# The V store of head 30 as an indexed GpSimd store without eight rows, and x and grad_out loaded to all partitions

## The chip, the cores and the metric

The kernel runs on one core of a Trainium2 chip. Five engines each work through their own list of instructions: TensorE (PE; its weight loads are shown as PEld), VectorE (DVE), ScalarE (ACT), GpSimd (POOL) and SyncE (SP). They are ordered only by semaphores. SyncE, ScalarE and GpSimd can each issue DMAs; all of these are carried by the same 16 DMA engines. In the profile the DMA packets of SyncE are queue q1, those of ScalarE q10, those of GpSimd q0.

The metric is the device time of one execution in microseconds, as the median of several runs. Beside it stands the profile of one execution. All times given as points in time are microseconds from the start of that execution's span.

## The reference, cut to what matters

The reference computes one decoding step of a transformer block, and the gradients of all its inputs. A layer-normed row x (640 numbers) goes through attention against a cache of 8192 keys and values for each of 32 heads, and beside it through a gated MLP. Cut and simplified:

```python
def _A_ref(x, k_cache, v_cache, wq, wo):
    q = (x @ wq).reshape(B, Sq, Hq, Dh).transpose(0, 2, 1, 3)
    scores = jnp.einsum("bhqd,bhkd->bhqk", q, k) * (Dh ** -0.5)
    p = _softmax(scores, axis=-1)
    o = jnp.einsum("bhqk,bhkd->bhqd", p, v)
    return o.transpose(0, 2, 1, 3).reshape(B, Sq, Hq * Dh) @ wo
...
def _B_ref(x, w1, w3, w2):
    h = _silu(x @ w1) * (x @ w3)
    return h @ w2
...
x = A_x
xn = _layernorm(x, axis=-1)
return x + _A_ref(xn, A_k_cache, A_v_cache, A_wq, A_wo) + _B_ref(xn, B_w1, B_w3, B_w2)
...
_out, _vjp = jax.vjp(_f, A_x, A_k_cache, A_v_cache, A_wq, A_wo, B_w1, B_w3, B_w2)
_grads = _vjp(grad_out)
return (_out, *_grads)
```

All tensors are bfloat16. The caches and their gradients have the shape (1, 32, 8192, 128): 2 MB for K and 2 MB for V of each head. With one query, the gradient of K of one head is the outer product of a vector over the 8192 positions with one over the 128 columns, and so is that of V. So the kernel must read 134 MB of caches and write 134 MB of their gradients; the weights and their gradients add some 17 MB each way (the page counts 151.34 MB read and as many written).

## The kernel before, in words

Head by head, one K tile and one V tile are loaded by SyncE (2 MB each, 128 partitions of 64 positions, that is 16 KB in one piece on each partition). TensorE transposes them in pieces (`T`, L305), ScalarE copies these out of PSUM (L307), TensorE multiplies them with q and with the head's part of the gradient (`Mp`, L324), and the scores and the gradient of the probabilities come out of small products (`selm`, L340). Softmax, then `o_sum` and `dq_sum` (L417) use the tiles once more. At last DVE overwrites the tiles in place with the outer products (`outer`, L450): `outer_v` with the gradient of V, `outer_k` with that of K. `store` (L461) sends the tile to HBM, gives its buffer back and calls `load_next`, which issues the next load if there is one.

There are ten such buffers (`NSLOT`). Four of them hold the MLP's weights in the first part of the run and join the others later. All loads and stores of K and V go through one function, `fifo` (L105), so they stand in one list on SyncE, in the order in which the code calls it; a store that waits for DVE holds back all that stand behind it.

The outer products of head h are made while head h+1 is computed: `outers_a(h)` makes the whole of V and stores it, and makes half of K; `outers_b(h)` makes the other half of K and stores it. So the last stores on SyncE are V28, K28, V29, K29, V30, K30, V31, K31 (a letter for the cache and the number of the head). The 64 loads have all been issued before V28 is stored.

Heads come in groups of four. The weights wq and wo of a group are loaded, and their gradients stored, by GpSimd (L111, L113, L495, L504). The last group's two stores (0.64 MB each) end the kernel together with K31, and four small stores of the output row and of x's gradient by ScalarE (L813).

At the start, x and grad_out are each loaded as one row into one partition (L99). TensorE turns them into columns (L219, L221) and spreads grad_out over all partitions (L223, L225); ScalarE copies that into `g_bc` (L227, L228). The mean and the variance of x are sums over a column and then over the partitions (L231 to L237). The normalised column `xn_col_bf` goes into the first q (`prep_q`, L260). `g_bc` goes into the first products with wo (`prep_do`, L251), for which the group's wo must have landed.

Nothing in the code says which instruction waits for which. A layer below it derives the waits from what each instruction reads and writes, tiles and tensors in HBM alike. DMAs are counted on a few semaphores in turn (lanes): eight for SyncE and ScalarE together, eight for GpSimd. A DMA that takes a lane first waits until the one before it on that lane has landed. The instructions stand on each engine in the order in which the code makes them.

Of the kernel before, what the change touches and what calls it, by code (L numbers as in the profile page):

```python
# [9 lines left out]
BF16 = mybir.dt.bfloat16  # L10
F32 = mybir.dt.float32
ALU = mybir.AluOpType
ACTF = mybir.ActivationFunctionType
AX = mybir.AxisListType
PSUM = bass.MemoryType.PSUM

P = 128
# [4 lines left out]
def kernel(  # L22
# [22 lines left out]
    nc = tc.nc  # L45
    H = A_k_cache.shape[1]
    SK = A_k_cache.shape[2]
    DH = A_k_cache.shape[3]
    D = A_x.shape[2]
    F = B_w1.shape[1]  # L50
    assert DH == P and D % P == 0 and SK % P == 0
    NC = D // P
# [5 lines left out]
    scale = float(DH) ** -0.5  # L58

    consts = ctx.enter_context(tc.tile_pool(name="consts", bufs=1))  # L60
    kvpool = ctx.enter_context(tc.tile_pool(name="kv", bufs=1))
    wpool = ctx.enter_context(tc.tile_pool(name="wp", bufs=3))
    tpool = ctx.enter_context(tc.tile_pool(name="tp", bufs=4))
# [12 lines left out]
    dkc = out_2.rearrange("b h (p j) d -> (b h) p (j d)", p=P)  # L76
    dvc = out_3.rearrange("b h (p j) d -> (b h) p (j d)", p=P)
# [14 lines left out]
    NSLOT = 10  # L92
    RW = 64

    rows_in = []
    for src in (A_x, grad_out):
        r_kt = tpool.tile([P, 4, P], F32, name="row_kt", tag="KT")
        row = r_kt[0:1].rearrange("p k w -> p (k w)").bitcast(BF16)[:, 0:D]
        nc.scalar.dma_start(row, src.rearrange("a b d -> (a b) d"))  # L99
        rows_in.append(row)  # L100
    x_row, g_row = rows_in
    g_bc = consts.tile([P, D], BF16, name="g_bc")

    def fifo(out_, in_):
        nc.sync.dma_start(out_, in_)  # L105
# [16 lines left out]
    def load_next():  # L122
        if not pending or len(free_slots) < lag[0]:
            return
        kind, h = pending.pop(0)
        t = free_slots.pop(0)
        fifo(t[:], (kc if kind == "K" else vc)[h])
        kv_tiles[(kind, h)] = t
# [33 lines left out]
    ident_f = consts.tile([P, P], F32, name="ident_f")  # L162
    make_identity(nc, ident_f[:])
    ident_bf = consts.tile([P, P], BF16, name="ident_bf")
    nc.vector.tensor_copy(ident_bf[:], ident_f[:])
    masks = consts.tile([P, 4], F32, name="masks")
    pm_one = masks[:, 0:2]
    nc.vector.memset(pm_one[:, 0:1], 1.0)
    nc.vector.memset(pm_one[:, 1:2], -1.0)
    ones_b = pm_one[:, 0:1].to_broadcast([P, P])  # L170
    negones_b = pm_one[:, 1:2].to_broadcast([P, P])
    one_bf = consts.tile([P, 1], BF16, name="one_bf")
    nc.vector.memset(one_bf[:], 1.0)
    eps_t = consts.tile([P, 1], F32, name="eps_t")
# [22 lines left out]
    negmean = consts.tile([P, 1], F32, name="negmean")  # L197
    rstd = consts.tile([P, 1], F32, name="rstd")
    x_col = consts.tile([P, NC], F32, name="x_col")
    g_col = consts.tile([P, NC], F32, name="g_col")  # L200
    xn_col = consts.tile([P, NC], F32, name="xn_col")
    xn_col_bf = consts.tile([P, NC], BF16, name="xn_col_bf")

    def kt_tile():
        return tpool.tile([P, 4, P], F32, name="KT", tag="KT")

    def t_tile():
        t = kt_tile()
        return t[:].rearrange("p k w -> p (k w)").bitcast(BF16)

    def pst():
        return ps_t.tile([P, 512], F32, name="pT", tag="pT")

    ln3 = consts.tile([P, 3], F32, name="ln3")
    xsum, sumsq, std = ln3[:, 0:1], ln3[:, 1:2], ln3[:, 2:3]
    ps_xg = pst()
    ps_g = pst()
    for ci in range(NC):
        nc.tensor.matmul(ps_xg[:, ci:ci + 1], lhsT=x_row[:, ci * P:(ci + 1) * P], rhs=one_bf[0:1, :],  # L219
                         start=True, stop=True)  # L220
        nc.tensor.matmul(ps_xg[:, NC + ci:NC + ci + 1], lhsT=g_row[:, ci * P:(ci + 1) * P], rhs=one_bf[0:1, :],  # L221
                         start=True, stop=True)
    nc.tensor.matmul(ps_xg[:, P:P + D - 512], lhsT=one_bf[0:1, :].to_broadcast([1, P]), rhs=g_row[:, 512:D],  # L223
                     start=True, stop=True)
    nc.tensor.matmul(ps_g[:], lhsT=one_bf[0:1, :].to_broadcast([1, P]), rhs=g_row[:, 0:512],  # L225
                     start=True, stop=True)
    nc.scalar.copy(g_bc[:, 0:512], ps_g[:])  # L227
    nc.scalar.copy(g_bc[:, 512:D], ps_xg[:, P:P + D - 512])  # L228
    nc.vector.tensor_copy(x_col[:], ps_xg[:, 0:NC])
    nc.vector.tensor_copy(g_col[:], ps_xg[:, NC:2 * NC])  # L230
    nc.vector.tensor_reduce(xsum, x_col[:], AX.X, ALU.add)  # L231
    nc.tensor.matmul(ps_xg[:, 16:17], lhsT=ones_b, rhs=xsum, start=True, stop=True)
    nc.vector.tensor_scalar(negmean[:], ps_xg[:, 16:17], -1.0 / D, None, ALU.mult)
    nc.vector.scalar_tensor_tensor(xn_col[:], x_col[:], negmean[:], x_col[:], ALU.add, ALU.mult, accum_out=sumsq)
    nc.tensor.matmul(ps_xg[:, 17:18], lhsT=ones_b, rhs=sumsq, start=True, stop=True)
    nc.scalar.activation(std, ps_xg[:, 17:18], ACTF.Sqrt, bias=eps_t[:], scale=1.0 / D)
    nc.vector.reciprocal(rstd[:], std)  # L237
    nc.vector.tensor_scalar(xn_col[:], x_col[:], negmean[:], rstd[:], ALU.add, ALU.mult)
    nc.vector.tensor_copy(xn_col_bf[:], xn_col[:])

    def prep_new(g):
# [29 lines left out]
    def prep_cm(g, ps):  # L271
        nc.vector.tensor_tensor(grp[g]["cm"][:].rearrange("p t a h m -> p (t a h) m"),
                                ps.unsqueeze(2).to_broadcast([P, 4 * GH, 2]),
                                mask2.unsqueeze(1).to_broadcast([P, 4 * GH, 2]), ALU.mult)

    hd = {}
    NCH = J // 8
# [183 lines left out]
    def store(kind, h):  # L461
        t = kv_tiles.pop((kind, h))
        if kind == "K":
            hd.pop(h)
        fifo((dkc if kind == "K" else dvc)[h], t[:])
        free_slots.append(t)
        load_next()

# [189 lines left out]
    def side_v(h):  # L658
        g, hh = divmod(h, GH)
        if hh == 0 and g > 0:  # L660
            fin_wo(g - 1)
        elif hh == 1 and g > 0:
            fin_wq(g - 1, 2)
        elif hh == 2 and g + 1 < NG:
            prep_new(g + 1)
            prep_do(g + 1, 0)
        elif hh == 3 and g + 1 < NG:
            prep_cm(g + 1, hd[h]["m"][:, 324:324 + 4 * GH])
# [13 lines left out]
    def outers_a(h):  # L682
        outer_v(h, 0, J // 2)
        outer_v(h, J // 2, J)
        store("V", h)
        outer_k(h, 0, J // 2)

    def outers_b(h):
        outer_k(h, J // 2, J)
        store("K", h)  # L690
# [73 lines left out]
    for hh in range(GH):  # L764
        prep_do(0, hh)
    prep_sel(0, ps_0[:, 8:8 + 4 * GH])
    prep_cm(0, ps_0[:, 8:8 + 4 * GH])
    fill_qz(0)
    rows_pe(0, ps_0[:, 64:64 + 2 * DH], False)
# [31 lines left out]
    nst = consts.tile([P, 2], F32, name="nst")  # L801
    nc.vector.tensor_scalar(nst[:], ps_f[:, 0:2], -1.0 / D, None, ALU.mult)
    t5 = consts.tile([P, NC], F32, name="t5")
    nc.vector.scalar_tensor_tensor(t5[:], xn_col[:], nst[:, 1:2], dxn[:], ALU.mult, ALU.add)
    nc.vector.tensor_scalar(t5[:], t5[:], nst[:, 0:1], rstd[:], ALU.add, ALU.mult)
    nc.vector.tensor_tensor(fin[:, NC:2 * NC], t5[:], g_col[:], ALU.add)
    ps_o = pst()
    nc.tensor.transpose(ps_o[0:2 * NC, 0:P], fin[:], ident_f[:])
# [35 lines left out]
```

## Time and profile before

| | |
|---|---|
| time, median of 3 runs | 732.48 us (732.37 to 733.36) |
| the profiled execution's own time | 732.37 us |
| its span | 730.6 us |
| busy: PE, PEld, DVE, ACT, POOL | 606.6, 423.1, 459.3, 369.4, 29.9 us |
| moved by DMA | 303.58 MB, 416 GB/s on the mean |
| share of SyncE's queue (q1), of GpSimd's (q0) in the DMA engines' time | 89.5%, 8.9% |
| stores of K and V, issue to landing, median | 31.1 us |
| loads of K, of V, issue to landing, median | 25.2, 26.3 us |

The span is what the profile covers; the time is that of the whole execution, 1.8 us more. "Busy" counts instructions that an engine works on. The DMA share is the mean busy share of the sixteen DMA engines in a stretch of time; it can be a little over 1, since packets overlap at their ends. "Issue to landing" is the time from the instruction that issues a DMA until the last of its sixteen parts is counted. In the lists of waits, a name with a q (SPq) is an engine's instruction list rather than its arithmetic.

### The profile page before, as it was taken

Reading aid. Unit: us, or ns where it says so; the run is one execution under the profiler, and the core shown is the slowest. Engines: PE = TensorE matmul, PEld = TensorE weight load, DVE = VectorE, ACT = ScalarE, POOL = GpSimd, SP = SyncE. Lnnn points to the kernel's source line nnn. Section 1 sums busy time; section 2 is a strip of 40 time slices with the busy share of each in tenths; the row PEclk is TensorE's granted clock in tenths of the full one; section 3 lists DMA queues with packets and bytes.
Section 4 is the critical chain, followed back from the end, with each engine's and each line's share of the span. In section 5 each row is a group of like instructions: output and inputs, shape, how many; then the busy total and the mean of one; then the engine's idle time right before and its main releaser. Section 6 shows DMA issues by size and latency. Waiting matters only on the chain.

```text
span 730.6 us, 13869 instructions
## 1 busy us (share of the span) xinstructions
PE 606.6 (83%) x5669; PEld 423.1 (58%) x5669; DVE 459.3 (63%) x806; ACT 369.4 (51%) x719; POOL 29.9 (4%) x45
## 2 busy tenths in 40 slices
PE   3989589998899889988987887888898889978940
PEld 2657466666566656666655555566566556655620
DVE  4069646677757776776646765547756756667482
ACT  2650736656556556554655554545554536655510
POOL 0010110000100000001000000000000000000000
PEclk9996699999999999988998998979897969989765
DMA  9999999999999999999999999999999999999993
GB/s 354 400 411 420 425 421 432 415 429 425 417 416 426 429 427 421 430 428 426 425 428 426 431 423 427 429 428 428 427 424 429 429 427 428 428 434 426 425 393 155
DMA packets 27145, 303.58 MB, mean 416 GB/s; under 512 B 2807, under 2 KB 4153, under 8 KB 10441
## 3 DMA queue, kind: packets, MB, share of 16 engines
q1 hardware_dynamic: 21328, 276.39, 89.5%
q0 software_dynamic: 5728, 26.30, 8.9%
q8 instruction: 44, 0.72, 0.4%
q14 instruction: 21, 0.16, 0.1%
q10 hardware_dynamic: 24, 0.01, 0.0%
HBM read 151.34 MB, written 151.34 MB: 414 GB/s over the span
## 4 chain that ended last, share of the span: by engine, by line
PE 42%; DMA 41%; DVE 8%; ACT 6%; issue 1%; SPq 0%; ACTq 0%; DVEq 0%
DMA out_dram<-kv 22%; PE pT L305 20%; DMA kv<-in_A_k_cache_dram 11%; DMA kv<-in_A_v_cache_dram 7%; PE m L340 6%; PE X L417 5%; ACT KT L307 4%; PE sA L324 4%; DVE kv L450 3%; PE dA L324 2%; DMA wo_g<-in_A_wo_dram 2%; DVE side L251 1%; PE gu_ps L527 1%; ACT KT L330 1%; PE m L430 1%
## 5 line engine op out<-in xcount | busy, mean ns | idle before, releaser
L307 ACT COPY KT<-pT 128x512 f32<-128x512 f32 x512 | 289.5, 589 | 235.3 <-PE pT L305 200.6
L305 PE MATMUL pT<-ident_f,kv 128*128 128x128 f32 x2048 | 318.7, 296 | 40.6 <-DMA kv<-in_A_k_cache_dram 17.9
L305 PEld LDWEIGHTS pT<-ident_f,kv 128*128 128x128 f32 x2048 | 248.5, 154 | 97.0 <-PE pT L305 27.8
L450 DVE TENSOR_TENSOR kv<-qd,U 128x4096 bf16<-128x4096 bf16 x64 | 146.0, 2284 | 0.0
L450 DVE TENSOR_TENSOR kv<-qd,P 128x4096 bf16<-128x4096 bf16 x64 | 143.6, 2284 | 0.0
L340 PEld LDWEIGHTS m<-selc,KT 128*128 128x128 f32 x512 | 67.4, 205 | 45.8 <-ACT KT L330 34.1
L340 PE MATMUL m<-selc,KT 128*128 128x16 f32 x512 | 73.2, 276 | 22.7 <-ACT KT L330 22.5
L417 PE MATMUL X<-kv,Z 128*32 128x512 bf16 x1024 | 85.3, 462 | 1.8 <-DVE Z L434 1.8
L400 DVE SCALAR_TENSOR_TENSOR U<-m,P 128x64 bf16<-128x64 f32 x32 | 7.4, 233 | 104.9 <-PE m L340 104.9
L324 PE MATMUL dA<-KT,qz 128*32 128x512 bf16 x512 | 55.2, 418 | 0.2 <-ACT KT L307 0.2
L324 PE MATMUL sA<-KT,qz 128*32 128x512 bf16 x512 | 55.1, 421 | 0.0
L324 PEld LDWEIGHTS <-qz 128*32 128x32 bf16 x1024 | 26.6, 93 | 42.8 <-issue 41.6
L417 PEld LDWEIGHTS <-Z 128*32 128x32 bf16 x1024 | 28.6, 110 | 33.9 <-issue 16.6
L366 DVE TENSOR_REDUCE mrow<-m 128x1 f32<-128x64 f32 x32 | 7.1, 223 | 62.9 <-PE m L340 62.9
L360 ACT CAST qd<-pT 128x256 bf16<-128x256 f32 x32 | 11.9, 372 | 48.6 <-DVE kv L450 32.4
L500 DVE SCALAR_TENSOR_TENSOR wq_g<-wq_g,side 128x512 bf16<-128x512 bf16 x40 | 27.3, 683 | 0.0
L251 DVE SCALAR_TENSOR_TENSOR side<-wo_g,g_bc 128x640 bf16<-128x640 bf16 x32 | 26.2, 819 | 1.1 <-DMA wo_g<-in_A_wo_dram 0.8
L373 DVE TENSOR_REDUCE negM<-m 128x1 f32<-128x128 f32 x32 | 9.3, 291 | 24.5 <-PE m L370 24.5
L432 DVE SCALAR_TENSOR_TENSOR U<-m,P 128x128 bf16<-128x128 f32 x32 | 11.4, 355 | 18.0 <-PE m L430 18.0
L390 DVE RECIPROCAL rZ<-m 128x1 f32<-128x1 f32 x32 | 5.3, 167 | 24.1 <-PE m L384 24.1
L330 ACT COPY KT<-dA 128x512 f32<-128x512 f32 x32 | 19.3, 604 | 0.6 <-PE dA L324 0.6
L330 ACT COPY KT<-sA 128x512 f32<-128x512 f32 x32 | 19.3, 603 | 0.0
(154 smaller groups left out, 365.2 us busy)
## 6 DMA issues: line engine op xcount, KB each, us to landing
out_dram<-kv SPq DMA_DIRECT2D x64, 2048.0 KB, 31.1
kv<-in_A_k_cache_dram SPq DMA_DIRECT2D x32, 2048.0 KB, 25.2
kv<-in_A_v_cache_dram SPq DMA_DIRECT2D x32, 2048.0 KB, 26.3
out_dram<-wo_g POOLq DMA_DIRECT2D x8, 640.0 KB, 11.4
out_dram<-wq_g POOLq DMA_DIRECT2D x8, 640.0 KB, 12.9
wq_g<-in_A_wq_dram POOLq DMA_DIRECT2D x7, 640.0 KB, 13.2
wo_g<-in_A_wo_dram POOLq DMA_DIRECT2D x7, 640.0 KB, 19.3
kv<-in_B_w_dram SPq DMA_DIRECT2D x2, 1728.0 KB, 28.7
```

The lines of the kernel that those rows point to most:

```text
L251: nc.vector.scalar_tensor_tensor(junk[:], G_["wo"][:, hh, :], 1.0, g_bc[:], ALU.mult, ALU.mult, accum_out=G_["do"][:, hh:hh + 1])
L305: nc.tensor.transpose(pT[:, k * P:(k + 1) * P], W3[:, 4 * c + k, :], ident_f[:])
L307: nc.scalar.copy(KT[:].rearrange("p k w -> p (k w)"), pT[:])
L324: nc.tensor.matmul(S_[kind][q:q + QW, :], lhsT=S_["qz"][:, o:o + QW], rhs=KTb[:, par, :], start=(c0 == 0), stop=(c0 == NCH - 2), skip_grou ...
L330: nc.scalar.copy(XS[:].rearrange("p k w -> p (k w)"), S_.pop(kind)[:])
L340: nc.tensor.matmul(S_["m"][:, b0:b0 + J].rearrange("p (c k t) -> p k c t", k=4, t=2)[:, k, :, :], lhsT=XS[:, k, :], rhs=selc[:].rearrange( ...
L360: nc.scalar.copy(qd[:].rearrange("p a d -> p (a d)"), hd[h].pop("ps_r"))
L373: nc.vector.tensor_reduce(S_["negM"][:], S_["m"][:, 2 * J:2 * J + P], AX.X, ALU.max, negate=True)
L417: nc.tensor.matmul(xg["X"][q:q + QW, :], lhsT=Z[:, o:o + QW], rhs=W[:, N4 * i:N4 * (i + 1)], start=(slot == 0 and i < 4), stop=(slot == NS ...
L432: nc.vector.scalar_tensor_tensor(S_["U2"][:], S_["V"][:, 0:J].unsqueeze(2).to_broadcast([P, J, 2]), S_["m"][:, OC + NS:OC + NS + 1], S_["P ...
L450: nc.vector.tensor_tensor(dst[:, lo * DH:hi * DH].rearrange("p (j a b) -> p j a b", a=DH // 2, b=2), vec.rearrange("p (a b) -> p a b", b=2 ...
L500: nc.vector.scalar_tensor_tensor(wq_g[:, ci, :], wq_g[:, ci, :], 1.0, dqb, ALU.mult, ALU.mult, accum_out=dxa[:, ci, g:g + 1])
```

## The change

Two things differ. First, x and grad_out are loaded by two DMAs that write the same row into all 128 partitions. The mean and variance of x are then sums along a row, made by DVE on all partitions alike; TensorE only makes the columns, and its broadcast of grad_out, ScalarE's two copies and the sums over partitions are gone.

Second, V30 is stored in another way. A list of 128 row numbers is made at the start: partition p gets 30*128 + p. For the partitions 32 to 39 a number of 2*32*128 = 8192 is added, which lies beyond the last row (4095). The store is then an indexed DMA of GpSimd, which writes partition p's 16 KB to the row of out_3 that its number names, and leaves out rows beyond the bound. The eight rows left out are stored by SyncE in two stores of four rows. K30, V31, K31 and all earlier stores stay as they were.

```diff
-    rows_in = []
-    for src in (A_x, grad_out):
-        r_kt = tpool.tile([P, 4, P], F32, name="row_kt", tag="KT")
-        row = r_kt[0:1].rearrange("p k w -> p (k w)").bitcast(BF16)[:, 0:D]
-        nc.scalar.dma_start(row, src.rearrange("a b d -> (a b) d"))
-        rows_in.append(row)
-    x_row, g_row = rows_in
+    x_kt = tpool.tile([P, 4, P], F32, name="x_kt", tag="KT")
+    x_bc_bf = x_kt[:].rearrange("p k w -> p (k w)").bitcast(BF16)[:, 0:D]
+    nc.scalar.dma_start(x_bc_bf, A_x.rearrange("a b d -> (a b d)").partition_broadcast(P))
     g_bc = consts.tile([P, D], BF16, name="g_bc")
+    nc.scalar.dma_start(g_bc[:], grad_out.rearrange("a b d -> (a b d)").partition_broadcast(P))
...
-    ln3 = consts.tile([P, 3], F32, name="ln3")
-    xsum, sumsq, std = ln3[:, 0:1], ln3[:, 1:2], ln3[:, 2:3]
+    ln3 = consts.tile([P, 4], F32, name="ln3")
+    msum, sumsq, std = ln3[:, 0:1], ln3[:, 1:2], ln3[:, 2:3]
+    nc.vector.tensor_reduce(msum, x_bc_bf, AX.X, ALU.add)
+    nc.vector.tensor_scalar(negmean[:], msum, -1.0 / D, None, ALU.mult)
+    nc.vector.scalar_tensor_tensor(t_tile()[:, 0:D], x_bc_bf, negmean[:], x_bc_bf, ALU.add, ALU.mult,
+                                   accum_out=sumsq)
+    nc.scalar.activation(std, sumsq, ACTF.Sqrt, bias=eps_t[:], scale=1.0 / D)
+    nc.vector.reciprocal(rstd[:], std)
     ps_xg = pst()
-    ps_g = pst()
     for ci in range(NC):
-        nc.tensor.matmul(ps_xg[:, ci:ci + 1], lhsT=x_row[:, ci * P:(ci + 1) * P], rhs=one_bf[0:1, :],
+        nc.tensor.matmul(ps_xg[:, ci:ci + 1], lhsT=x_bc_bf[0:1, ci * P:(ci + 1) * P], rhs=one_bf[0:1, :],
                          start=True, stop=True)
-        nc.tensor.matmul(ps_xg[:, NC + ci:NC + ci + 1], lhsT=g_row[:, ci * P:(ci + 1) * P], rhs=one_bf[0:1, :],
+        nc.tensor.matmul(ps_xg[:, NC + ci:NC + ci + 1], lhsT=g_bc[0:1, ci * P:(ci + 1) * P], rhs=one_bf[0:1, :],
                          start=True, stop=True)
-    nc.tensor.matmul(ps_xg[:, P:P + D - 512], lhsT=one_bf[0:1, :].to_broadcast([1, P]), rhs=g_row[:, 512:D],
-                     start=True, stop=True)
-    nc.tensor.matmul(ps_g[:], lhsT=one_bf[0:1, :].to_broadcast([1, P]), rhs=g_row[:, 0:512],
-                     start=True, stop=True)
-    nc.scalar.copy(g_bc[:, 0:512], ps_g[:])
-    nc.scalar.copy(g_bc[:, 512:D], ps_xg[:, P:P + D - 512])
     nc.vector.tensor_copy(x_col[:], ps_xg[:, 0:NC])
     nc.vector.tensor_copy(g_col[:], ps_xg[:, NC:2 * NC])
-    nc.vector.tensor_reduce(xsum, x_col[:], AX.X, ALU.add)
-    nc.tensor.matmul(ps_xg[:, 16:17], lhsT=ones_b, rhs=xsum, start=True, stop=True)
...
-    nc.tensor.matmul(ps_xg[:, 17:18], lhsT=ones_b, rhs=sumsq, start=True, stop=True)
...
+    SCAT = (H - 2,)
+    R0, NR = 32, 8
+    dvc_rows = out_3.rearrange("b h (p j) d -> (b h p) (j d)", p=P)
+    sidx = masks[:, 4:5].bitcast(mybir.dt.int32)
+    nc.gpsimd.iota(sidx, pattern=[[0, len(SCAT)]], base=SCAT[0] * P, channel_multiplier=1)
+    skip = ln3[:, 3:4]
+    nc.vector.tensor_reduce(skip, ident_f[:, R0:R0 + NR], AX.X, ALU.add)
+    nc.vector.scalar_tensor_tensor(sidx, skip.to_broadcast([P, len(SCAT)]), float(2 * H * P), sidx,
+                                   ALU.mult, ALU.add)
...
-        fifo((dkc if kind == "K" else dvc)[h], t[:])
+        dst = (dkc if kind == "K" else dvc)[h]
+        if kind == "V" and h in SCAT:
+            i = SCAT.index(h)
+            nc.gpsimd.indirect_dma_start(
+                out=dvc_rows, out_offset=bass.IndirectOffsetOnAxis(ap=sidx[:, i:i + 1], axis=0),
+                in_=t[:], in_offset=None, bounds_check=H * P - 1, oob_is_err=False)
+            for r0 in range(R0, R0 + NR, 4):
+                fifo(dst[r0:r0 + 4], t[r0:r0 + 4])
+        else:
+            fifo(dst, t[:])
         free_slots.append(t)
         load_next()
```

More of the change, by code (lines that the diff above doesn't have):

```diff
@@ L165 @@
     nc.vector.tensor_copy(ident_bf[:], ident_f[:])
-    masks = consts.tile([P, 4], F32, name="masks")
+    masks = consts.tile([P, 8], F32, name="masks")
     pm_one = masks[:, 0:2]
@@ L230 @@
     nc.vector.tensor_copy(g_col[:], ps_xg[:, NC:2 * NC])
-    nc.vector.tensor_reduce(xsum, x_col[:], AX.X, ALU.add)
-    nc.tensor.matmul(ps_xg[:, 16:17], lhsT=ones_b, rhs=xsum, start=True, stop=True)
-    nc.vector.tensor_scalar(negmean[:], ps_xg[:, 16:17], -1.0 / D, None, ALU.mult)
-    nc.vector.scalar_tensor_tensor(xn_col[:], x_col[:], negmean[:], x_col[:], ALU.add, ALU.mult, accum_out=sumsq)
-    nc.tensor.matmul(ps_xg[:, 17:18], lhsT=ones_b, rhs=sumsq, start=True, stop=True)
-    nc.scalar.activation(std, ps_xg[:, 17:18], ACTF.Sqrt, bias=eps_t[:], scale=1.0 / D)
@@ L237 @@
-    nc.vector.reciprocal(rstd[:], std)
-    nc.vector.tensor_scalar(xn_col[:], x_col[:], negmean[:], rstd[:], ALU.add, ALU.mult)
+    nc.vector.tensor_scalar(xn_col[:], x_col[:], negmean[:], rstd, ALU.add, ALU.mult)
     nc.vector.tensor_copy(xn_col_bf[:], xn_col[:])
@@ L804 @@
     nc.vector.scalar_tensor_tensor(t5[:], xn_col[:], nst[:, 1:2], dxn[:], ALU.mult, ALU.add)
-    nc.vector.tensor_scalar(t5[:], t5[:], nst[:, 0:1], rstd[:], ALU.add, ALU.mult)
+    nc.vector.tensor_scalar(t5[:], t5[:], nst[:, 0:1], rstd, ALU.add, ALU.mult)
     nc.vector.tensor_tensor(fin[:, NC:2 * NC], t5[:], g_col[:], ALU.add)
```

## The prediction

> **What bounds the kernel now.** I read the page's slices first, then the windows, then the DMA view of single stores, then what SyncE waits for at the end. The slices:
>
> ```profile
> span 730.6 us, 13869 instructions
> ...
> PE   3989589998899889988987887888898889978940
> ...
> DMA  9999999999999999999999999999999999999993
> ```
>
> The DMA engines are full from the first slice to the last but one; no compute engine is. So what counts is DMA work added, DMA work taken off the engine that ends last, and DMA time left empty. Windows, whose last two columns are the DMA share and GB/s:
>
> ```profile
> 500.00:700.00 200.00, 175.04 (x1555) 119.23 (x1553) 123.86 (x205) 103.22 (x207) 5.76 (x7) 0.88 1.00 426
> ...
> 694.00:698.00 4.00, 3.51 (x38) 1.94 (x36) 2.98 (x6) 1.27 (x3) 0.00 (x0) 1.00 0.76 317
> ...
> 718.00:720.00 2.00, 0.07 (x1) 0.00 (x0) 0.28 (x1) 0.00 (x0) 0.00 (x0) 0.50 0.57 222
> 720.00:722.00 2.00, 0.00 (x0) 0.00 (x0) 0.00 (x0) 0.00 (x0) 0.00 (x0) 0.50 0.23 95
> 722.00:724.00 2.00, 0.00 (x0) 0.00 (x0) 0.00 (x0) 0.00 (x0) 0.00 (x0) 0.50 0.06 25
> ...
> 726.00:728.00 2.00, 0.00 (x0) 0.00 (x0) 0.00 (x0) 0.00 (x0) 0.00 (x0) 0.50 0.07 31
> ```
>
> From 722 on the share is 0.06 to 0.07, and 1/16 is 0.063: one DMA engine of sixteen works alone for some 7 us. Call it the late engine; it sets the end, and it is what skipping eight rows could relieve. Eight rows of 16 KB are one engine's part of a 2 MB store: 2.097 MB at 426 GB/s, 4.9 us.
>
> How late it is in the middle of the tail shows in single stores. The timeline has SyncE issuing V29 at 665.28, K29 at 674.04, V30 at 686.01, K30 at 696.85, V31 at 703.12 and K31 at 707.52 (V29 is the V store of head 29). The DMA view, one window round each of V29, K29 and K31; the last column is us to landing on all engines:
>
> ```profile
> out_dram<-kv SPq DMA_DIRECT2D x1, 2048.0 KB, 36.9
> ...
> out_dram<-kv SPq DMA_DIRECT2D x1, 2048.0 KB, 32.8
> ...
> out_dram<-kv SPq DMA_DIRECT2D x1, 2048.0 KB, 22.1
> ```
>
> So V29 lands at 702.2, K29 at 706.8, K31 at 729.6. Yet at 694 to 698 a quarter of the engines are already empty (share 0.76), though V29, K29 and V30 are all issued by then: most engines are far ahead, and a landing is the late engine's. SyncE's last waits agree: it is released by the small output rows, then the last wq store, then K31:
>
> ```profile
> SPq L839 <- DMA out_dram<-fin_bf: 11.6, 1, 11.6
> SPq L839 <- DMA out_dram<-wq_g: 9.4, 1, 9.4
> ...
> SPq L839 <- DMA out_dram<-kv: 0.4, 1, 0.4
> ```
>
> From 707.9 that is 719.5, 728.9 and 729.3. The rows also price a small SyncE-type store: issued at 718.42, landed at 719.5, so 1.1 us of latency without data (about 0.8 before the data, the rest after).
>
> The price of a GpSimd DMA's start comes from the last wo store, issued at 710.04. From 710.0 to 713.9 the DMA view has no packet of its queue; to 714.1 it has five:
>
> ```profile
> 710.04 0.77 POOL L495 DMA_DIRECT2D out_dram<-wo_g  x1 [38.48 <-DVE wo_g L494]
> ...
> q0 software_dynamic: 5, 0.03, 1.6%
> ```
>
> That is 3.9 us from issue to first packet.
>
> **The change, part by part.**
>
> *The loads.* Two loads of one row (2.5 KB) become two of 128 rows, 0.33 MB in all. In the window 0 to 18 us DMA runs at 352 GB/s: 0.9 us. From below 0, if they fit in the emptiness that leaves that window's share at 0.91; from above 3.2, if they repeat the whole start-up loss (18 us at 352 instead of 428 GB/s). I take 0.9, the same bytes at the rate of that stage; as the engines are full from there to the tail, all that follows shifts by it.
>
> *The start on the compute engines.* Two PE broadcasts of grad_out, their ScalarE copies (0.58 and 0.27), two column sums on PE and their DVE steps go; DVE gets two passes over 128x640 (0.82 each by the row of L251, same shape). I cost this at nothing. The cover: DVE's first prep_do starts at 12.88, when wo_g has landed, and PE waits for its fourth until 16.57, while the q product that needs xn ends at 12.95. So the new chain may be 3.6 us later, and the wider grad_out load too. If that cover goes, the first V store (41.69) slips, but the loads issued before it are 20.5 MB, some 50 us of DMA, so another 8 us lie under it. The iota, the reduction of the skip column and the index sum are three tiny instructions in the same stretch: nothing.
>
> *The scatter.* Here the order of the built program decides. The scatter names the whole of out_3 (4096 rows) as its output, since indices choose the rows. So its issue on GpSimd carries waits for the landing counts of V27, V28 and V29, beside the one for DVE. The first four-row SyncE store waits for the scatter's landing, K31 for the first four-row store's. And SyncE issues in order: K30, V31 and K31 stand behind the four-row store. Before, V30 waited for DVE alone. Step by step:
>
> 1. V29 lands at 702.2, with the loads 703.1. The other fifteen engines ran dry at about 690 to 700.
> 2. First scatter packet 3.9 later: 707.0. An indexed store isn't in this trace. Below: 3.9, as plain 128-row, 512-row and 640-row GpSimd DMAs spend only 0.56 to 0.88 on issue; above: 6.5, were the issue to take four times the longest. I take the row of the plain one.
> 3. Eight rows on each engine, 4.9, and 0.4 to land: 712.3. If rows 32 to 39 aren't the late engine's, that engine ends K29 at 707.7 and then does its eight: 713.0.
> 4. SyncE issues two four-row stores and then K30, 0.33 each (its row) with gaps: 0.85; 0.8 to data: 713.95. Two rows each on four engines are 1.2, of which 0.75 fits before K30: 714.4. (Bounds 0 and 1.2.)
> 5. K30, V31 and K31, 6.29 MB at 426 GB/s, are 14.8; the last wo and wq stores, 1.31 MB, are 3.1. They are issued near 711 and 716 and start 3.9 later, so no gap takes them: 732.3. Landed: 732.7.
>
> Before, 729.6. The sum is +3.1 on the profiled execution's 732.37 (span 730.6 and 1.8 around it), which is 0.1 under the median 732.48: 735.5. The 7 us of one lone engine at the end do go, because everyone starts K30 together; but they are bought with about 11 us (695.5 to 707) in which most engines have nothing to store, and 2 us more between scatter and K30.
>
> GpSimd's own queue loses nothing: behind the scatter stands the wo store, not ready before 710.9. ScalarE's four last stores wait for lanes that landed long before.
>
> [...] The row for the start is 3.9 us. [...]
>
> [...] No row here tells which engine takes which partition.
>
> **Rivals.**
>
> *Not slower, short start.* The wait is there, but an indexed store's packets come quicker than a plain one's. [...] It decides when the start is under about 2.3. For it: only that the form is new. Against it: the wo store's 3.9.
>
> *Faster, no late V29.* If the late engine's lag is a chance of the profiled run, V29 lands when the fifteenth engine is done, near 695, and the whole chain starts 7 us earlier: 728.4. Against it: the three runs lie within 1 us. The relief without any wait (4.9 less, 0.9 more: 728.4) would need the scatter issued by 697, and the build says no.
>
> *Slower still.* Indexed descriptors are made row by row on GpSimd, slower than 0.88 for 640 rows, or are held while DVE runs the 2.28 us products of L450, which fill 703 to 708 just then. Price: the delay itself, 3 us give 738.5. Against it: plain GpSimd issues beside L450 took no longer than others.
>
> *The start shows.* The broadcasts hold x back by over 3.6 us and more than the 8 us of queued loads: each us beyond counts once, 737.5 with 2. Against it: both covers.
>
> **How the numbers follow.** Forecast 0.72; slower still 0.12; start shows 0.03; short start 0.10; no late V29 0.03. A measurement of this kernel can't tell 0.2% (1.5 us) from no change. Faster by more 0.03 (no late V29); within 0.10 (short start); slower 0.87 (the rest). The range: 733.8 (loads free, four-row stores hidden, start 0.35 shorter) to 738.7 (start 6.5, loads at 1.5), with some 0.1 left out on each side.
>
> **What will show it.** In the profile after: a stretch of several us round 700 to 707 where the DMA share falls to 0.1 or less; GpSimd's issue waiting for a DMA until 702 to 704; first packets of its queue about 4 us later; SyncE waiting some 25 us for the scatter, then three 2 MB stores in one run to the end; no lone engine in the last windows. The DMA share stays full from 2 to 690. If the share never drops before the scatter, or the scatter starts before 700, my step 1 is wrong; if the gap is there but longer than 4 us, step 2.

## The result and the profile after

| | before | after |
|---|---|---|
| time, median | 733.2 us (6 runs, 732.37 to 733.7) | 739.62 us (6 runs, 738.6 to 741.22) |
| ratio, 95% interval | | 1.0091 (1.0077 to 1.0105) |
| the profiled execution: time, span | 732.37, 730.6 us | 738.6, 736.8 us |

The changed kernel is slower by 6.4 us; 3.1 had been forecast, with a range up to 738.7. So the direction was right and the size was not. Both profiled executions are the fastest of their six runs; between them lie 6.2 us, and the medians lie 0.8 and 1.0 higher.

The slices of the profile after:

```profile
span 736.8 us, 13860 instructions
...
DMA  9999999999999999999999999999999999999758
GB/s 338 404 408 423 424 423 429 417 427 424 416 419 427 429 424 423 428 428 428 424 427 431 427 426 426 427 430 428 425 427 429 428 430 428 427 429 429 322 206 335
```

Only the first slice is clearly lower than before (338 GB/s, 354 before); the next 36 are within 5 GB/s of before. Nearly all of the loss is in the last three. The windows after, whose last two columns are the DMA share and GB/s:

```profile
694.00:698.00 4.00, 3.50 (x38) 1.93 (x35) 2.97 (x6) 1.26 (x3) 0.00 (x0) 1.00 0.52 219
698.00:702.00 4.00, 2.57 (x24) 1.81 (x24) 3.87 (x4) 0.59 (x1) 0.00 (x0) 0.82 0.21 90
702.00:706.00 4.00, 0.40 (x2) 0.30 (x2) 4.00 (x3) 0.17 (x1) 2.23 (x1) 0.50 0.07 29
706.00:710.00 4.00, 1.12 (x24) 1.03 (x24) 3.19 (x8) 0.59 (x1) 0.24 (x1) 0.50 0.86 356
...
714.20:716.40 2.20, 0.40 (x2) 0.43 (x2) 1.58 (x10) 0.00 (x0) 0.87 (x1) 0.50 0.25 58
...
734.00:736.80 2.80, 0.00 (x0) 0.00 (x0) 0.00 (x0) 0.00 (x0) 0.00 (x0) 0.50 0.07 29
```

There are two holes. The first, from 695 to 706.8, was forecast: most engines have stored all that they had, and the scatter waits for the late engine's part of V29. The second was not: at 714.2 to 716.4 the share is 0.25, four engines of sixteen. In the last stretch three engines still store after the other thirteen have ended; before, one engine worked alone for some 7 us.

GpSimd's timeline, and the DMA view in windows round the issues of V29 (at 666.78) and of the scatter, with the us to landing at the end:

```profile
703.77 2.47 POOL L467 DMA_INDIRECT out_dram<-kv,masks  x1 [30.70 <-DVE kv L449]
```

```profile
out_dram<-kv SPq DMA_DIRECT2D x1, 2048.0 KB, 35.9
...
out_dram<-kv,masks POOLq DMA_INDIRECT x1, 9.5
```

V29 lands at 702.7, the scatter is issued at 703.8 and has landed at 713.3. The page puts the wait of 30.7 us before it down to DVE. But in the kernel before, where V30's store waited for DVE alone, it was issued at 686.0, and in the trace GpSimd's wait for V29's counter ends at 702.74, 0.03 after V29's landing; so it was the wait for V29 that lasted. GpSimd then spent another 1.0 us on its remaining waits. SyncE's waits after:

```profile
SPq L102 <- DMA out_dram<-kv,masks: 37.4, 1, 37.4
...
SPq L847 <- DMA out_dram<-wq_g: 10.3, 1, 10.3
...
SPq L847 <- DMA out_dram<-kv: 5.7, 2, 4.8
```

SyncE stands 37.4 us before the first four-row store, until 713.3, with K30, V31 and K31 behind it. Last come the wq store and K31. What the second hole is shows in the DMA view of 714.0 to 716.3:

```profile
q1 hardware_dynamic: 4, 0.07, 25.2%
```

Four packets of 16 KB, the first four-row store, fill 25.2% of 16 engines' 2.3 us: 9.3 us, or 2.3 us a row. A row of a full store takes 0.61. In the trace the second four-row store's rows took 0.6, 1.5, 2.3 and 2.5 us, and K30's first packets on the other twelve engines started at 716.35. That these twelve had nothing until then is a matter of K30's issue on SyncE, which took 1.41 us instead of the usual 0.33:

```profile
714.44 1.41 SPq L102 DMA_DIRECT2D out_dram<-kv  x1
```

At the end twelve engines have landed K31 at 733.4 to 733.6 and four at 734.0, 735.4, 735.6 and 735.9: those that carried the eight rows, by all appearances, though the trace doesn't name engines.

### The profile page after: what moved, and what is told of

It reads as the page before. It is cut to its first block, busy times and chain, and to the rows that moved or that the text cites. A ratio compares the mean times of both kernels' runs of the same rounds, so it can differ in the third digit from the quotient of the medians.

```text
span 736.8 us, 13860 instructions
## 1 busy us (share of the span) xinstructions
PE 602.0 (82%) x5663; PEld 421.4 (57%) x5663; DVE 460.8 (63%) x808; ACT 368.0 (50%) x716; POOL 32.6 (4%) x47
## 4 chain that ended last, share of the span: by engine, by line
DMA 53%; PE 31%; DVE 6%; ACT 5%; issue 1%; SPq 0%; ACTq 0%; DVEq 0%
DMA out_dram<-kv 37%; PE pT L304 16%; DMA kv<-in_A_k_cache_dram 11%; PE m L339 5%; ACT KT L306 4%; DMA kv<-in_A_v_cache_dram 4%; PE X L416 3%; PE sA L323 3%; DVE kv L449 3%; PE dA L323 2%; DMA wo_g<-in_A_wo_dram 2%; DVE side L240 1%; ACT KT L329 1%; PE m L383 1%; PE m L429 1%
## 5 line engine op out<-in xcount | busy, mean ns | idle before, releaser
L416 PE MATMUL X<-kv,Z 128*32 128x512 bf16 x1024 | 83.4, 454 | 1.8 <-DVE Z L433 1.8
```

What stands on the lines that cost most here:

```text
L416: nc.tensor.matmul(xg["X"][q:q + QW, :], lhsT=Z[:, o:o + QW], rhs=W[:, N4 * i:N4 * (i + 1)], start=(slot == 0 and i < 4), stop=(slot == NS ...
```

## The experiments

The theory after this profile, an assumption of the author's: the four rows of one such store lie next to each other and are read out of SBUF through one way, called a port in the expectations below, so four engines share what one has otherwise. No run shows a port; what the runs show is the time that a row took. Against the theory stood that the wait for V29, the indexed store itself, or the loads are what costs. A second question was whether eight rows can be taken off the late engine at a gain at all, since in the changed kernel that engine had kept its share. In the table, us is the ratio less one, times 733.

| kernel | median us | ratio, 95% interval | us |
|---|---|---|---|
| changed kernel | 739.62 | 1.0091 (1.0077 to 1.0105) | +6.7 |
| before, with the new loads alone | 734.21 | 1.0009 (1.0000 to 1.0018) | +0.7 |
| changed, scatter of all 128 rows, no four-row stores | 733.95 | 1.0007 (0.9998 to 1.0015) | +0.5 |
| changed, no wait for V27 to V29 | 735.05 | 1.0018 (1.0007 to 1.0028) | +1.3 |
| changed, the four rows four partitions apart | 736.15 | 1.0035 (1.0022 to 1.0048) | +2.6 |
| changed, four-row stores behind K31 | 736.48 | 1.0050 (1.0031 to 1.0069) | +3.7 |
| changed, rows 16 to 19 and 48 to 51 | 742.82 | 1.0135 (1.0117 to 1.0154) | +9.9 |
| before, relief of the late engine at V30 | 731.45 | 0.9976 (0.9966 to 0.9986) | -1.8 |
| before, relief at V16 | 729.91 | 0.9963 (0.9947 to 0.9978) | -2.7 |
| before, relief at V16 and K16 | 731.63 | 0.9987 (0.9973 to 1.0001) | -1.0 |
| before, relief at V16, four-row stores earlier | 729.14 | 0.9943 (0.9929 to 0.9956) | -4.2 |

**The loads alone.** The kernel before with the change's loads and its new start, all stores as before:

```diff
-        nc.scalar.dma_start(row, src.rearrange("a b d -> (a b) d"))
...
+    nc.scalar.dma_start(x_bc_bf, A_x.rearrange("a b d -> (a b d)").partition_broadcast(P))
...
+    nc.scalar.dma_start(g_bc[:], grad_out.rearrange("a b d -> (a b d)").partition_broadcast(P))
```

> The kernel before with the two 128-row loads of x and grad_out and the statistics on DVE, but with V30 stored as before. Theory A (the loads cost their bytes, about 1 us; the rest of the change's 6.4 us lies in the tail: a gap because the scatter waits for V29, and the two four-row stores): 733.2 + 0.6 to 1.0, so 733.8 to 734.2. Rival C (most of the loss is at the start: x landed at 9.75 us and grad_out at 10.6, several us later than before): 737 or more.

Measured 734.21, +0.7 with an interval from 0 to 1.3. In the changed kernel's trace V29 landed 0.6 later than before, which agrees. So the start costs about its bytes, and nothing beyond them shows.

**The scatter without four-row stores.** The changed kernel; no index is pushed out of bounds, so the scatter takes all 128 rows:

```diff
-    nc.vector.scalar_tensor_tensor(sidx, skip.to_broadcast([P, len(SCAT)]), float(2 * H * P), sidx,
+    nc.vector.scalar_tensor_tensor(sidx, skip.to_broadcast([P, len(SCAT)]), 0.0, sidx,
...
-            for r0 in range(R0, R0 + NR, 4):
-                fifo(dst[r0:r0 + 4], t[r0:r0 + 4])
```

> The changed kernel without the skipping: the scatter stores all 128 rows, the two four-row stores are gone, and so is what stands behind them: K30 goes when DVE is done, V31 and K31 still stand behind the scatter's landing. The scatter still waits for V29. Theory A: K30 fills part of the gap; the scatter lands on the late engine near 717.4 (K30's and its own eight rows by turns from 707), V31 and K31 then take 12.5 us: last landing near 730.4 instead of 735.9, so 733.5 to 735. Rival (the wait for V29 alone makes the loss, with or without the four-row stores): 738 to 740.

Measured 733.95, +0.5: not more than the loads by themselves. GpSimd's timeline and the DMA view of the scatter in this run:

```profile
703.68 2.68 POOL L467 DMA_INDIRECT out_dram<-kv,masks  x1 [28.17 <-DMA out_dram<-kv]
```

```profile
out_dram<-kv,masks POOLq DMA_INDIRECT x1, 13.8
```

The scatter waits for V29 here as well, until 703.7, and lands at 717.5, later than in the changed kernel. But K30 no longer stands behind it: SyncE issues K30 at 697.0, and the fifteen other engines store it while the scatter waits. V31 does wait for the scatter (issued at 717.9), and most engines stand idle once more before that (a share of 0.35 from 714 to 718); the end comes at 730.96 all the same, since V31 and K31 then run on all engines together and the lone engine's stretch at the end is gone. So the wait and the indexed store cost nothing on balance, at most about 1 us by the interval; what costs is what is hung on them.

**The changed kernel without the wait for V27 to V29.** The heads are renumbered (head h works on the cache of head h XOR 30), so that the scatter's target is the first head's 128 rows and is named as these alone; no other store writes there.

```diff
-        fifo(t[:], (kc if kind == "K" else vc)[h])
+        fifo(t[:], (kc if kind == "K" else vc)[h ^ HX])
...
-    dvc_rows = out_3.rearrange("b h (p j) d -> (b h p) (j d)", p=P)
+    dvc_rows = dvc[SCAT[0] ^ HX]
```

> The changed kernel with the heads renumbered (h exclusive-or 30 on every access to HBM), so that the head stored by the scatter is the first in HBM, and the scatter's output can be named as that head's 128 rows alone. The work and the order stay; only the scatter's waits for the landings of V27 to V29 go. Theory A: the scatter is issued at about 687 instead of 703.8, SyncE is free again near 701, and the late engine, which still has its eight rows, sets the end with the same work as before plus the loads: 733.8 to 735. If the skipped rows were the late engine's after all: 729 to 730.5. Rival B (an indexed store and what follows it are slow by themselves, whatever they wait for): 737 to 740.

Measured 735.05, +1.3, at the upper edge of theory A. GpSimd's timeline, and the DMA view of the scatter:

```profile
689.92 2.86 POOL L469 DMA_INDIRECT out_dram<-kv,masks  x1 [13.98 <-DVE kv L451]
```

```profile
out_dram<-kv,masks POOLq DMA_INDIRECT x1, 17.0
```

The scatter goes out at 689.9 instead of 703.8 and lands at 706.9, 6.4 us earlier, the first four-row store as much, and K30 3.5 us earlier (710.9). So the wait takes part in the 6.4 us, but only as the first link of the chain scatter, four-row stores, K30; the run before showed that without the later links it is free on balance.

**Four partitions apart.** The changed kernel, with rows 32, 36, 40, ... 60 left out instead of 32 to 39, so that the four partitions of one store lie four apart:

```diff
-            for r0 in range(R0, R0 + NR, 4):
-                fifo(dst[r0:r0 + 4], t[r0:r0 + 4])
+            for r0 in range(R0, R0 + 4 * NR, 16):
+                fifo(dst[r0:r0 + 16:4], t[r0:r0 + 16:4])
```

> The changed kernel, but the eight rows left out and stored by SyncE are 32, 36, 40 and so on to 60, in two stores of four rows, instead of 32 to 39. Everything else, the waits too, stays. Theory A (four rows of neighbouring partitions share one way out of the SBUF, so that the four DMA engines that carry them took 2.3 to 2.4 us for a row instead of 0.61): rows at 0.6 to 0.7 us, and the end earlier by the 2.4 us by which four engines ended after the other twelve, up to 1 us more where K30 starts earlier: 736 to 737.3. Rival (a store of four rows is slow by itself): 739 to 740.

Measured 736.15, +2.6. The same view as above, round the first four-row store of this run (713.3 to 714.4, 1.1 us):

```profile
q1 hardware_dynamic: 4, 0.07, 14.0%
```

14.0% of 16 times 1.1 us is 2.46 us for four packets, 0.62 us a row where the changed kernel has 2.3. The bytes, the number of rows and the waits are those of the changed kernel; the scatter, which leaves out other rows, lands 8.9 us after its issue (9.5 there). The stores land 2.4 us after their issue, K30 is issued at 714.42 as in the changed kernel (714.44), but the issue is short, and its first packets start at 715.27 instead of 716.35:

```profile
714.42 0.34 SPq L102 DMA_DIRECT2D out_dram<-kv  x1
```

All sixteen engines land K31 within 0.3 us, the last at 732.67 instead of 735.91. This shows that the place of the four rows sets the price, and that both the later start of K30 and the late end of four engines go with it. With the partitions the rows' places in HBM changed too (64 KB apart instead of side by side), so this run alone doesn't say on which side the price arises; later runs bear on that.

**The late engine, and its eight rows.** To find the late engine's rows, the kernel before was run with its last output rows stored five at a time instead of three, two, four and one, and with two extra stores of 16 and 8 rows behind them (they repeat what has been stored already):

```diff
-    for dst, r0, cuts in ((out_0, 0, (0, 3, 5)), (out_1, NC, (0, 4, 5))):
+    for dst, r0, cuts in ((out_0, 0, (0, 5)), (out_1, NC, (0, 5))):
```

> The kernel before; at the end the output row and x's gradient go out in one store of five rows each, and some 5 us later, when only the late engine should still be at work, rows of wo's gradient that are in HBM already are written there once more, in one store of 16 rows and one of 8. One look at how the parts of these small stores land tells which engine is late. Theory A: the 1-, 2-, 3- and 4-row stores of the kernel before met no backlog, so the late engine is none of the first four: in the 16-row store one part of sixteen lands 0.3 us or more after the others; the 8-row store and the five-row stores tell whether it is one of the first eight, and whether it is the fifth. If the lateness is not one engine's, the parts land together, or several are late. The time: 732.5 to 735.

Time 734.75, a single run, beside 732.8. In its trace the five-row stores, issued at 719.19 and 719.51, landed four parts at 720.3 to 720.7 and the fifth at 724.0 and 725.5. In the kernel before, the same rows in stores of up to four landed with no late part (719.51 to 719.54, 720.12 to 720.18 for the longer ones). So, if such stores take the engines in the same order, the fifth is the late one. The store of eight rows had another late part besides (725.6 and 728.1, six at 723.8 to 723.9), so the fifth isn't the only engine that lags. The author took it that partitions are dealt out by fours, which no run had shown by then; the fifth engine's would be 16 to 19 and 48 to 51. These were left out in the next run, in place of 32 to 39, all else as in the changed kernel:

```diff
-    R0, NR = 32, 8
+    ROWS4 = (16, 48)
...
-            for r0 in range(R0, R0 + NR, 4):
+            for r0 in ROWS4:
                 fifo(dst[r0:r0 + 4], t[r0:r0 + 4])
```

> The changed kernel, but the rows left out are 16 to 19 and 48 to 51 instead of 32 to 39, sent by two four-row stores at the same place with the same waits. In the earlier run with five-row stores the late engine took the fifth row, and if partitions are dealt to engines by fours, 16 to 19 and 48 to 51 are its whole share. Theory A (the scatter frees an engine only if its whole share is named, and the late engine had kept its share in the changed kernel): the scatter lands near 712.3 rather than 713.3, with no part of it on the late engine; the four-row stores still take some 2.4 us a row; time 738.0 to 739.0. Rival (these are not the late engine's rows): one engine has no part of the scatter, but it still lands near 713.3; 739.6.

Measured 742.82: the expected 1 us of gain became a loss of 3. The scatter did what was expected, in the DMA view round its issue at 703.47:

```profile
out_dram<-kv,masks POOLq DMA_INDIRECT x1, 7.8
```

It landed at 711.2, 2.1 us earlier than in the changed kernel. In the trace one of its sixteen parts is done at 707.54, just behind that engine's part of K29 (707.36), and the rest at 711.04 to 711.22: the late engine had none of its rows. In the changed kernel two parts were done early (709.62 and 709.64), thirteen at 712.15 to 712.28 and the late engine's at 713.32. The two early parts were 2.5 to 2.7 us ahead of the thirteen, about four rows at 0.61. So rows 32 to 39 are half the share of each of two engines, and neither is the late one; 16 to 19 and 48 to 51 are the whole share of one, the late one.

The four-row stores are what was missed. The same view of the first one (711.9 to 714.4, 2.5 us):

```profile
q1 hardware_dynamic: 4, 0.07, 36.6%
```

That is 14.6 us over four, 3.7 a row; in the trace the rows of the second store, together with K30's, took 4.6 to 5.0 us each, and SyncE was held by its issues (K30 2.26 us, V31 4.95, where 0.33 is usual). A fifth engine, which landed K30 at 724.4 between the eleven (720.5) and the four (728.4 to 729.6), had rows of 1.1 to 1.2 us in that time. Four engines landed K31 at 738.8 to 739.8, eleven at 732.1 to 732.2 and one at 735.9. So a row took 0.62 us with the partitions four apart, 2.3 in the first store of 32 to 39, and 3.7 to 5.0 with 16 to 19 and 48 to 51, though in the last of these runs the wo store ran at the same time (103 packets in that window, 3 in the changed kernel's). Why these eight rows were dearer than 32 to 39 was not shown.

**The four-row stores behind K31.** The changed kernel, the two stores moved to the end of SyncE's list:

```diff
-            for r0 in range(R0, R0 + NR, 4):
-                fifo(dst[r0:r0 + 4], t[r0:r0 + 4])
+            rows4.append((dst, t))
...
     outers_b(H - 1)
+    for dst4, t4 in rows4:
+        for r0 in range(R0, R0 + NR, 4):
+            fifo(dst4[r0:r0 + 4], t4[r0:r0 + 4])
```

> The changed kernel with one thing moved: the two four-row stores of V30 go out behind K31 instead of ahead of K30. The scatter, its wait for V27 to V29, the rows left out and the loads are the same; K30 is no longer held by the scatter, V31 still is. Theory A (the four-row stores are dear because K30, V31 and K31 stand behind them on SyncE and on the ports they read through): K30 issued near 697, V31 near 714 to 718, and the time is that of the run with the scatter of all rows, 733.95, plus at most the four-row rows at the end of four engines: 733.5 to 736. Rival (eight rows in four-row stores cost their 4 us wherever they stand): 738 to 740.

Measured 736.48, +3.7, half a us above the range of the theory and well below the rival's. K31 has landed on all engines at 731.7, and after that only the eight rows are left, under two engines' worth of work (0.11 of sixteen) at 22 GB/s:

```profile
732.00:735.00 3.00, 0.00 (x0) 0.00 (x0) 0.00 (x0) 0.00 (x0) 0.00 (x0) 0.50 0.11 22
```

They end at 735.0, 3.3 us after K31. In the trace the rows of the first of the two took 2.2 to 2.4 us here too, with hardly any other store in hand. Ahead of K30 the same two stores cost some 3 us more (6.7 less 3.7), since K30 then waits for the scatter as well and everything behind them starts later.

**Relief alone.** The last question: is it worth anything to take rows off the late engine? The kernel before with its own loads, heads renumbered as above, V30 as a scatter without rows 16 to 19 and 48 to 51, and the four-row stores behind K31:

```diff
+        if h == HX and kind in SCAT:
+            nc.gpsimd.indirect_dma_start(
+                out=dst, out_offset=bass.IndirectOffsetOnAxis(ap=sidx, axis=0),
+                in_=t[:], in_offset=None, bounds_check=P - 1, oob_is_err=False)
+            rows4[(kind, h)] = (dst, t)
+        else:
+            fifo(dst, t[:])
```

> The kernel before with its own loads of x and grad_out; heads renumbered so that the scatter names 128 rows only and waits for no store. V30 (the second last head) is a scatter without rows 16 to 19 and 48 to 51, the late engine's share; these go as two four-row SyncE stores behind K31, where they hold nothing back. The relief alone. If eight rows taken off the late engine are worth their time there (4.9 us of full rate): about 729. Rival (what is late is the port that these partitions are read through, or the four-row stores at 2.4 us a row end later themselves): 733 to 735.

Measured 731.45, -1.8: between the two. The late engine landed its part of V31 at 718.3 but needed 9.0 us more for its eight rows of K31, where the kernel before needed 6.0; in the trace three rows of K31, one after another, took 1.2 us each (719.2 to 723.6) while rows of the four-row stores were in hand, and the rows of the other engines 0.61. So 3.0 us of the relief was given back, and why was not shown. That rows of K31 were slow too speaks against a slow place in HBM, since K31 goes to another tensor than V30. But not all rows beside such a store were slow: beside the first four-row store (714.3 to 717.9), whose own rows took 2.2 to 4.0 us, no row of V31 or K31 took over 0.63. What the slow rows share stays open.

Then the same with head 16, the four-row stores ahead of V17's:

```diff
-    HX = 30
+    HX = 16
...
+        if (kind, h - 1) in rows4:
+            send_rows4(kind, h - 1)
```

> The same relief in the middle of the run: V of head 16 is the scatter without the late engine's eight rows, and the two four-row stores go ahead of V17's store. There the engines alternate loads and stores. If the late engine is only behind and every row off it brings its end forward: 729 to 731.5 (4.9 us less, a part of it lost to the four-row stores, which block two groups of four engines for up to 10 us of reading through one port). If the relief does not work, or the second latest engine is as late: 733 to 735.

Measured 729.91, -2.7, in the range of the relief that works. In the last windows of this run the lone stretch is shorter. The shares of the four windows of 2 us from 720 on are 0.43, 0.14, 0.08 and 0.04; before had 0.23, 0.06, 0.07 and 0.07. The first two:

```profile
720.00:722.00 2.00, 0.00 (x0) 0.00 (x0) 0.00 (x0) 0.00 (x0) 0.00 (x0) 0.50 0.43 176
722.00:724.00 2.00, 0.00 (x0) 0.00 (x0) 0.00 (x0) 0.00 (x0) 0.00 (x0) 0.50 0.14 57
```

K16 treated likewise, sixteen rows in all:

```diff
-    SCAT = ('V',)
+    SCAT = ('V', 'K')
```

> As the run before, with V and K of head 16 both without the late engine's rows (sixteen rows moved). If the relief adds up: 726 to 730, bounded by the second latest engine, which ended its part of the last store some 5 to 7 us ahead of the latest. If relief in the middle gives nothing: 733 to 736.

Measured 731.63, between the two expectations: the second relief takes away more than it gives. It costs in the middle. From 437 to 455 and from 455 to 473 the kernel before moved 428 and 427 GB/s, the run with V16 alone 375 and 401, and this run 389 and, in the second window, 319. Eight packets of 16 KB took 2.2 to 2.8 us there (440 to 461), as the four-row stores' rows did at the end of a run. The second window of this run:

```profile
455.00:473.00 18.00, 16.87 (x183) 12.17 (x183) 11.91 (x21) 11.25 (x24) 0.76 (x1) 1.00 0.87 319
```

What the run with V16 alone had lost there began with a stall: its four-row stores, issued at 428.7, landed at 450.9, and the next load into their buffer was issued right after, at 451.0:

```profile
448.00:452.00 4.00, 4.00 (x36) 2.22 (x29) 4.00 (x3) 1.81 (x4) 0.00 (x0) 0.68 0.66 273
```

So the stores were moved ahead of K16's, two loads earlier:

```diff
-        if (kind, h - 1) in rows4:
-            send_rows4(kind, h - 1)
+        if kind == "K" and ("V", h) in rows4:
+            send_rows4("V", h)
```

> The run with the relief at head 16, V alone, with one thing moved: the two four-row stores go ahead of K16's store instead of V17's, one store and two loads earlier on SyncE. In that run they were issued at 429 and landed at 451, and the next load into their buffer waited for them; in 448 to 452 the DMA share was 0.66. If that stall is what the four-row stores cost there (0.34 of 4 us is 1.4 us): about 728.5 to 729.5. If the loss is the rows' slow reading itself: again 729.9.

Measured 729.14, ratio 0.9943 (0.9929 to 0.9956). The same window of this run, with the stall gone:

```profile
448.00:452.00 4.00, 4.00 (x36) 2.17 (x29) 4.00 (x3) 1.85 (x4) 0.00 (x0) 0.68 1.00 417
```

This version is 4.2 us faster than the kernel before, and the fastest of all that ran; its interval overlaps that of the first run with V16 (0.9947 to 0.9978), so the gain from moving the stores is not clear of noise. In the last stores of K and V the sixteenth part landed 3.0 to 4.0 us behind the fifteenth, against 5.8 to 9.3 in the kernel before. No run had the indexed store there with all its rows, so the relief isn't separated from the rest of that edit. Nor were rows slow here: while the two four-row stores were in hand (418.1 to 437.4), among the loads and stores of a full stretch, no packet of 16 KB took over 1.3 us.

## Why the prediction was wrong where it was, point by point

*The loads and the start.* Forecast +0.9 and hidden; measured +0.7 (0 to 1.3) with both. Right within the noise.

*Step 1, the wait for V29.* Right: the scatter waited for V29's landing at 702.7 (703.1 forecast), and the share fell to 0.07 before it.

*Step 2, the start.* Right in its sum only, by luck. The issue came 1.1 us after V29's landing and took 2.47 us, 2.5 times the longest plain one of the kernel before (0.99; the 0.88 of the prediction missed that one); the packets began 3.0 after the issue, not 3.9. First packets at 706.8, forecast 707.0. The 3.9 came from a DMA that was issued to full engines (share 1.00 from 710 to 714). The wq store of the same trace, issued at 715.18 (share 0.84 from 714 to 718), had its first packet after 1.5, and plain GpSimd DMAs of other runs whose engines had room took 1.4 to 1.8. The rest is what the rival "slower still" named, a hold by DVE. In all ten indexed stores of these runs whose issue began under one of DVE's outer products, the issue ended 0.94 to 0.96 us after that product, wherever in it the issue had begun; in the seven of them at the end of a run the first packet came 1.5 after it. In the run without the wait, for instance, the product ends at 691.83 and the issue, begun at 689.92, at 692.78:

```profile
689.54 2.29 DVE L451 TENSOR_TENSOR kv<-qd,U 128x4096 bf16<-128x4096 bf16 x1
```

In the changed kernel the product under way at the issue ended 1.5 us after it had begun, and 1.5 more makes the 3.0. Plain issues beside such products weren't held, as the prediction says: in the kernel before they took 0.77 to 0.88.

*Step 3, the scatter's landing.* 713.3 instead of the 712.3 taken. Its second case, that rows 32 to 39 aren't the late engine's (713.0), was the one that held. In the trace the parts done early, at 709.62 and 709.64, are two others than the late engine's, at 713.32.

*Step 4, the four-row stores.* This is the step that failed. It put two rows each on four engines at 1.2 us, that is 0.61 a row, the row of a full store; a row of the first store took 2.3 us, and its upper bound (1.2 with none hidden) excluded that. It was mis-sized twice. K30's packets began at 716.35 instead of 714.4, of which 1.0 is step 3's and the rest K30's long issue. And the four engines, with two slow rows each and K30 behind them, ended up to 2.3 us after the other twelve; the forecast had no such end. With the four rows four apart, and the same chain, the time was 736.15, against 735.5 forecast.

*Step 5, the run to the end.* Forecast 18.3 us from K30's first packet to the last landing; measured 17.2 on twelve engines and 19.6 on the four. From 732.7 to 735.9, then: 1.0 of step 3, 1.0 of K30's later start, 1.2 of the four engines. The other 1 us to the median of 739.62 is the profiled execution's: it was the fastest of six, as the one before was (0.8 under its median, where the prediction took 0.1 from three runs).

*The rivals.* No short start (3.0 us from issue to first packet), no earlier V29 (702.7). "The relief without any wait" was put at 728.4, a full share of 4.9 us; with the right rows and the stores out of the way it measured 729.14 without the loads, so that sum, 727.5 with the loads taken off, was not far out, though for eight other rows and at another place.

## What to carry to other kernels

A DMA of few partitions was not always as fast here as its number of engines: at the end of a run, four neighbouring partitions took 2.3 us a row and four that lie four apart 0.62, so spread them or keep such stores out of a queue in which anything stands behind them. A wait that a new store brings was cheap here as long as little was ordered behind it (+0.5 us with the scatter of all rows, the loads in it); count what its followers hold up, not the wait. A price read off a trace holds for the state in which it was paid: a start of 3.9 us behind full engines was 1.5 with room on them. And before rows are moved to relieve an engine, find out which rows are that engine's: rows 32 to 39 left the late engine its whole share, the right eight in the middle of the run were worth 2.7 to 4.2 us.

## What the runs showed of the hardware that was not expected

- Neighbouring partitions: 2.3 us for a row of 16 KB in a four-row store, 0.62 with the partitions four apart, 3.7 to 5.0 with 16 to 19 and 48 to 51. In the middle of the run, in the two runs with V16 alone, no row of such a store took over 1.3.
- The late engine is the one that, by all appearances, takes the fifth row of a five-row store (724.0 and 725.5, the other four at 720.3 to 720.7) and rows 16 to 19 and 48 to 51 of a full one. The last part of V29 landed 5.7 us after the fifteenth in the changed kernel, and 7.1 us before. Why it is late is open.
- SyncE's issues of K30 and V31 took 1.4 and 2.2 us while four engines had slow rows in hand, 2.3 and 5.0 with the slowest rows, and 0.34 and 0.35 with the rows four apart. K31's took 1.2, 1.7 and 1.45 in these three runs, and at the start of the kernel before, with loads queued, single issues took up to 4.4; that some engines' queues were full is likely, but was not shown.
- An indexed GpSimd store spent 1.2 to 2.9 us on its issue, against 0.5 to 1.0 for plain ones. Where a DVE product over 128x4096 was running when it began, it ended 0.95 us after that product, and at the end of a run the first packet came 1.5 after it. Why the product holds it was not shown.
